# Row sums and weight norms in PSUM, and an f32 low rank stage for two attentions

## The chip, the cores and the metric

One core of one Trainium2 chip. The metric is the device time of one execution in microseconds (us), the median of the runs. The core has TensorE (matmuls; PE in the rows, and PEld for its weight loads), VectorE (DVE), ScalarE (ACT), GpSimd (POOL) and SyncE (SP), whose queue issues the DMAs here. Each of them takes its instructions in order. [...]

## The reference

Three blocks in a row, in f32, on a batch of 4, 448 positions and 768 channels (12 heads of 64):

```python
x = attention(q, k, v)                        # causal softmax(q k^T / 8) v, 12 heads
xt = x.transpose(0, 2, 1)                     # "moe": low rank mixing of the positions, then an MLP
u = x + (xt @ U @ V).transpose(0, 2, 1)       # U (448, 32), V (32, 448)
x = u + np.maximum(u @ w_ch1, 0) @ w_ch2      # 768 -> 3072 -> 768
# "moe2": gate, top 2 of 4 experts; an expert is a causal attention of one head of 64, times wo
out = sum_e gate[e] * (softmax(q_e k_e^T / 8) v_e) @ wo[e]
```

## The kernel before

Positions are cut into NC = 4 chunks of C = 112, channels into KD = 6 blocks of 128, so that a block is a pair of heads. Accuracy comes from pairs of f16 numbers: an operand is cut into a high part and a rest, and a product is three f16 matmuls (`PASS`: high by high, high by rest, rest by high). The scores q k^T are f32 matmuls.

An attention (`attention(b)`, batch b) runs over its six pairs of heads, n = 6 b + p. For each: `softmax` forms the scores, takes row maxima under the mask on VectorE, exponentials with their row sums on ScalarE (`SUS`, 112 x 8: two heads by four chunks), cuts the result into high part (ScalarE) and rest (GpSimd), and transposes both by two DMA transposes. `weighted` calls `shares`, in which VectorE turns the eight sums per row into reciprocals, cuts these into two f16 parts and TensorE spreads them over the 64 rows of each head; then it multiplies the probabilities with v, and VectorE scales the product by the shares: y, 128 channels by 448 positions, in X3. ScalarE and GpSimd cut y into `XHL`, for the low rank stage.

`lowrank(n)`, issued a pair later: a DMA transpose turns XHL into XTR (positions in the partitions), twelve f16 matmuls of 128 columns multiply it by `U3` (U in high part and rest, three copies side by side, 96 columns), ScalarE scales the result out of the bank, VectorE subtracts on 32 of the 96 partitions, so that high part and rest stand above each other, and one f16 matmul by `VST` gives the addend, which VectorE adds to X3. For b = 0 the sum is cut into UH and UL at once.

Weights of the MLP arrive as f64; `weight_pair` decodes two tiles with integer operations on VectorE (three of 768 elements per tile), squares them on ScalarE, sums the squares with one f32 matmul into a bank (`norm`, 128 x 2), forms a power of two from it in four small VectorE operations and cuts the tiles, with two GpSimd subtractions of 384 columns each per tile. The MLP itself (`mlp(g, bs)`) runs in four groups of weights; the line `ORDER` says in which order attentions (a), MLP groups (m), joint groups (s) and experts (e) are written: a0 m00 a1 m01 m101 m20 m30 e0 a2 and so on.

All operations are first collected in `Program` and given a key; `plan` simulates the engines and issues the ready operation with the smallest key on each, after `SHIFTS` moved the keys of each part. Up to a fixed time, and at the end, it fills planned gaps of TensorE with dummy matmuls (`prog.idle`, L1346, 448 columns into bank 7) that keep its clock up; nothing uses their result.

`psum(kind)` hands out banks in turn: "b" (shares) and "l" (low rank) both take banks 3 and 4, "o" (weighted) bank 2, "r" (norm) bank 7, "s" (scores) 0 and 1. Every operation is recorded through one helper, so that nearly all instructions carry its line, L365; they are told apart by engine, operation and shape.

Of the kernel before, what the change touches and what calls it, by code (L numbers as in the profile page):

```python
# [20 lines left out]
NP = H // 2  # L21
# [347 lines left out]
def kernel(  # L369
# [96 lines left out]
    XHL = [view("xhl", i * 2048, 128, F16, 1024).rearrange("p (l s) -> p l s", l=2) for i in range(2)]  # L466
# [3 lines left out]
    U3 = view("u3", 0, 128, F16, 2 * NC * 3 * R).rearrange("p (l c r) -> p l c r", l=2, c=NC)  # L470
# [53 lines left out]
    def bits(a):  # L524
        return a.bitcast(I32)
# [127 lines left out]
    def shares(y, coef=None):  # L653

        i = heads[0] // 2 % 2
        su, rc = SUS[1 - i], RCH[1 - i]
        dve.tensor_scalar(su, su, EPS, 1.0 / RSC, op0=ALU.add, op1=ALU.mult)
# [7 lines left out]
        t = psum("b")  # L665
# [8 lines left out]
    def weighted(vs, pts, y, dst, coef=None, kind="o"):  # L674
# [13 lines left out]
        act.activation(dst[:, 0, 0:S], y, AF.Copy)  # L688
        pool.tensor_tensor(out=dst[:, 1, 0:S], in0=y, in1=dst[:, 0, 0:S], op=ALU.subtract)

    def lowrank(n):
        b, p = divmod(n, NP)
        iv = IV[:, b:b + 1]
        tst = TST
        sp.dma_start_transpose(out=XTR, in_=XHL[n % 2].rearrange("p l s -> p (l s)"))
        t = psum("l")
        with prog.group():
            for c in range(NC):
                for i, (lu_, lx) in enumerate(PASS):
                    mm(t[0:96, 0:128], U3[:, lu_, c], XTR[:, 4 * lx + c], c == 0 and i == 0, c == NC - 1 and i == 2)  # L700
# [74 lines left out]
    def attention(b):  # L775
        if b == B - 1:
            prog.key = HT * 30
            zero_pads(SLOTS[b][1][2:])
        if not b:
            prog.key = HT * 0.4  # L780
            v_scale(b)
            bound(CAP, SCAP, PV[:, 0:1])
# [486 lines left out]
    for a in XHL:  # L1269
        dve.memset(a[:, :, S:512], 0.0)  # L1270
# [122 lines left out]
```

## Time and profile before

| | |
|---|---|
| median of 3 runs | 1044.56 us (1044.13 to 1045.81) |
| profiled execution | 1046.19 us, of which the span of the trace is 1044.5 |
| granted clock of TensorE, mean | 0.994 |
| busy: TensorE, VectorE, ScalarE, GpSimd | 1024.4 (98%), 692.0 (66%), 613.6 (59%), 458.5 us (44%) |
| dummy matmuls among TensorE's | 383, 85.2 us |
| DMA | 192.53 MB, 88 DMA transposes |

The durations of the rows come from the one profiled execution, so they add up to its span and not to the median. A matmul's row shows its whole way through the array; how fast matmuls follow each other is read from the starts of neighbouring rows. In the rows "arena" is SBUF, "bank" PSUM, and out<-in (shape<-shape) are an instruction's operands; an f32 matmul has two records.

### The profile page before, as it was taken

The page shows a single profiled execution, that of the slowest core. Times are in us where ns is not written, and L with a number is a line of the kernel's source. Part 1 is how long each engine was busy: PE and PEld are TensorE (multiplying, and loading weights), DVE is VectorE, ACT ScalarE, POOL GpSimd, SP SyncE. Part 2 cuts the span into 40 slices and gives each one's busy share as a digit, 9 for nine tenths or more (in the row PEclk, how much of TensorE's full clock was granted, in tenths as well). Part 3 has the DMA queues.
Part 4 walks back from the last instruction along what each step waited for, and adds up shares of the span by engine and source line. Part 5 has one row for each costly group of instructions (what it writes and reads, how often), then busy time and mean ns, then how long its engine had stood idle before and what let it go on. Part 6 is the DMA issues. An engine that isn't in the chain of part 4 may idle for free.

```text
span 1044.5 us, 18607 instructions
## 1 busy us (share of the span) xinstructions
PE 1024.4 (98%) x6724; PEld 543.7 (52%) x6724; DVE 692.0 (66%) x1744; ACT 613.6 (59%) x1470; POOL 458.5 (44%) x500
## 2 busy tenths in 40 slices
PE   9999999999998999999999999999999999999998
PEld 4454555555544445644555644455555555655554
DVE  8888899876767677555647556488655677522363
ACT  6899886657744563668662569674552632722173
POOL 3777763343433331235540137567796891310011
PEclk9999999999998999999999999999999999999999
DMA  9999998566787887269994269893435445453024
GB/s 245 225 219 237 239 246 259 182 233 232 254 289 259 278 299 265 80 155 224 236 251 118 70 158 214 218 194 112 132 100 166 136 136 163 109 136 106 18 75 102
DMA packets 220139, 192.53 MB, mean 184 GB/s; under 512 B 176304, under 2 KB 179504, under 8 KB 220048
## 3 DMA queue, kind: packets, MB, share of 16 engines
q1 hardware_dynamic: 220048, 191.36, 68.1%
q8 instruction: 52, 0.85, 0.3%
q14 instruction: 39, 0.32, 0.1%
HBM read 112.16 MB, written 36.18 MB: 142 GB/s over the span
## 4 chain that ended last, share of the span: by engine, by line
PE 58%; DMA 4%; ACT 1%; POOL 1%; DVE 1%; issue 0%; SPq 0%; ACTq 0%; POOLq 0%
PE bank L365 58%; DMA arena<-arena 2%; ACT arena L365 1%; DMA out_dram<-arena 1%; DMA arena<-in_v_dram 1%; POOL arena L365 1%; DVE arena L365 1%; PE bank L1346 0%; ACT bank L365 0%; SPq L365 0%; ACTq L365 0%; POOLq L365 0%
## 5 line engine op out<-in xcount | busy, mean ns | idle before, releaser
L365 PE MATMUL bank<-arena 128*128 128x448 f16 (+12 forms) x6341 | 949.5, 326 | 14.6 <-ACT arena L365 7.8
L365 POOL TENSOR_TENSOR arena<-arena 128x384 f16<-128x384 f32 (+8 forms) x493 | 457.5, 949 | 575.0 <-ACT arena L365 506.6
L365 PEld LDWEIGHTS <-arena 128*128 128x128 f16 (+4 forms) x5853 | 473.5, 105 | 407.6 <-issue 62.6
L365 ACT ACTIVATE arena<-arena 128x448 f16<-128x448 f32 (+12 forms) x872 | 476.9, 585 | 214.7 <-DVE arena L365 122.1
L365 DVE SCALAR_TENSOR_TENSOR arena<-arena 128x768 int32<-128x768 int32 (+7 forms) x193 | 176.7, 930 | 6.3 <-ACT arena L365 5.0
L365 DVE TENSOR_TENSOR arena<-bank,arena 128x448 f16<-128x448 f32 (+2 forms) x160 | 95.5, 600 | 109.3 <-ACT arena L365 87.3
L365 DVE CUSTOM_DVE_ANT_0 arena<-bank,arena 112x112 f32<-112x112 f32 (+4 forms) x280 | 124.2, 477 | 62.5 <-PE bank L365 52.1
L365 DVE SCALAR_TENSOR_TENSOR arena<-bank,arena 128x448 f32<-128x448 f32 (+1 forms) x138 | 84.7, 621 | 66.1 <-PE bank L365 59.1
L365 DVE TENSOR_SCALAR arena<-arena 128x1 f32<-128x1 f32 (+11 forms) x305 | 81.7, 294 | 44.3 <-ACT arena L365 17.8
L365 ACT ACTIVATE bank<-bank,arena 128x448 f32<-128x448 f32 x72 | 43.1, 599 | 105.0 <-PE bank L365 105.0
L365 ACT ACTIVATE arena<-bank 128x448 f16<-128x448 f32 (+2 forms) x148 | 76.0, 518 | 48.3 <-PE bank L365 47.1
L365 DVE TENSOR_TENSOR arena<-arena 112x8 f16<-112x8 f32 (+10 forms) x136 | 86.2, 647 | 26.4 <-ACT arena L365 24.5
L1346 PE MATMUL bank<-arena 128*128 128x448 f16 x383 | 85.2, 360 | 1.8 <-DVE arena L1263 1.0
L365 ACT ACTIVATE arena<-bank,arena 128x448 f32<-128x448 f32 (+2 forms) x73 | 33.0, 458 | 57.9 <-PE bank L365 53.0
L365 PEld LDWEIGHTS bank<-arena 64*112 64x112 f32 (+4 forms) x488 | 39.6, 171 | 46.4 <-issue 16.7
L365 DVE TENSOR_REDUCE arena<-arena 128x1 f32<-128x448 f32 (+8 forms) x107 | 57.3, 545 | 5.7 <-DMA arena<-in_v_dram 2.3
L1346 PEld LDWEIGHTS <-arena 128*128 128x128 f16 x383 | 35.4, 101 | 42.7 <-issue 15.0
L365 ACT ACTIVATION_READ_ACCUMULATOR arena<-arena 112x1 f32 (+1 forms) x304 | 57.3, 188 | 0.0
L365 DVE DVE_READ_ACCUMULATOR2_ANT arena<- 112x1 f32 (+1 forms) x280 | 23.0, 82 | 0.0
L365 DVE CAST arena<-arena 112x8 f16<-112x8 f32 x32 | 9.0, 285 | 3.0 <-PE bank L365 2.7
L365 DVE TENSOR_SCALAR arena<-bank 128x2 f32<-128x2 f32 x24 | 3.7, 153 | 9.4 <-PE bank L365 9.3
L365 DVE RECIPROCAL arena<-arena 112x8 f32<-112x8 f32 (+1 forms) x36 | 7.0, 195 | 0.6
(11 smaller groups left out, 13.8 us busy)
## 6 DMA issues: line engine op xcount, KB each, us to landing
arena<-w SPq DMA_DIRECT2D x138, 384.0 KB, 3.4
arena<-in_w_dram SPq DMA_DIRECT2D x48, 768.0 KB, 5.5
w<-arena SPq DMA_DIRECT2D x78, 384.0 KB, 5.0
arena<-in_qk_dram SPq DMA_DIRECT2D x24, 448.0 KB, 4.8
arena<-in_v_dram SPq DMA_DIRECT2D x24, 224.0 KB, 4.6
out_dram<-arena SPq DMA_DIRECT2D x24, 224.0 KB, 2.1
arena<-in_we_dram SPq DMA_DIRECT2D x6, 384.0 KB, 6.4
arena<-arena SPq DMA_TRANSPOSE x88, 4.8
```

Source lines behind the costliest of these rows:

```text
L365: fn(*a, **k)
L1346: prog.idle = lambda late: nc.tensor.matmul(bank[:, 0 if late else 7, 64:512], ZERO.to_broadcast([128, 128]), ZERO.to_broadcast([128, S]), ...
```

## The change

- `norm`: the first and the third of the four small VectorE operations on the weight norm write the bank instead of SBUF, and the second and the fourth read it.
- `shares`: the bank for the spread shares is claimed first, and columns 448 to 455 of it hold the eight sums per row from the first VectorE operation on; the reciprocal, the product with the gates' weights, the cast and the subtraction read them there.
- For b < 2 (`lowrank32`): no cut of y into XHL, no DMA transpose, no U3. TensorE transposes y in four f32 matmuls against the identity, ScalarE copies the bank into `XNF` (112 x 512, f32); four f32 matmuls by U (`UF`, 32 columns) accumulate, ScalarE copies 32 x 128 to `TSF`, one f32 matmul by V (`LV`) gives the addend. The end of the stage (`finish`) is as before. For b >= 2 the stage stays f16, with 112 instead of 128 partitions.
- U is loaded in four blocks of 112 rows and not 128; the pads of XHL are zeroed ahead of attention 2 and not at the start; UF, LV and TSF lie where the expert weights `wv` come later, not in the ring of weight tiles.
- `SHIFTS` has new values, so the order of all engines' instructions is new.

```diff
@@ -49,31 +49,29 @@
 NT = 2 * NG * GF + NE
 MOVABLE = 270000.0
 SHIFTS = (
...
 )
 PASS = [(0, 0), (0, 1), (1, 0)]
 
@@ -463,11 +461,15 @@
         (P32[0:3], PHL[0:2], PT[0:3]),
         (P32[0:3], PHL[0:2] + [hslot("hid", 10752 + 5120 * i) for i in range(2)], PT[0:3]),
     ]
-    XHL = [view("xhl", i * 2048, 128, F16, 1024).rearrange("p (l s) -> p l s", l=2) for i in range(2)]
+    XHL = [view("xhl", i * 2048, 128, F16, 1024).rearrange("p (l c x) -> p l c x", l=2, c=NC) for i in range(2)]
+    XNF = [view("xhl", i * 2048, C, F32, 512) for i in range(2)]
+    LV = view("wv", 0, 96, F32, S)
+    UF = view("wv", 1792, C, F32, NC * R)
+    TSF = [view("wv", 2304 + 512 * i, R, F32, 128) for i in range(2)]
     XTR = view("xtr", 0, 128, F16, 1024).rearrange("p (k e) -> p k e", k=8)
     TST = view("tst", 0, 96, F16, 128)
     MASK = view("mask", 0, C, BF16, S)
-    U3 = view("u3", 0, 128, F16, 2 * NC * 3 * R).rearrange("p (l c r) -> p l c r", l=2, c=NC)
+    U3 = view("u3", 0, C, F16, 2 * NC * 3 * R).rearrange("p (l c r) -> p l c r", l=2, c=NC)
     ID = view("id", 0, 128, F16, 128)
     IDF = view("idf", 0, 128, F32, 128)
     ONE = view("one", 0, 128, F32, 128)
@@ -653,8 +655,10 @@
     def shares(y, coef=None):
 
         i = heads[0] // 2 % 2
-        su, rc = SUS[1 - i], RCH[1 - i]
-        dve.tensor_scalar(su, su, EPS, 1.0 / RSC, op0=ALU.add, op1=ALU.mult)
+        rc = RCH[1 - i]
+        t = psum("b")
+        su = t[0:C, S:S + 8]
+        dve.tensor_scalar(su, SUS[1 - i], EPS, 1.0 / RSC, op0=ALU.add, op1=ALU.mult)
         dve.reciprocal(su, su)
         if coef is not None:
             v = su.rearrange("p (h c) -> p c h", h=2)
@@ -662,7 +666,6 @@
         su = su.rearrange("p (h c) -> p h c", h=2)
         dve.tensor_copy(rc[:, 0], su)
         dve.tensor_tensor(out=rc[:, 1], in0=su, in1=rc[:, 0], op=ALU.subtract)
-        t = psum("b")
         with prog.group():
             for c in range(NC):
                 for l in range(2):
@@ -685,24 +688,54 @@
                            pt[0:C, k:k + kc * (NC - 1 - j) + 1:kc],
                            i == 0 and j == 0, i == 2 and j == NC - 1)
         dve.tensor_tensor(out=y, in0=t[:, 0:S], in1=y, op=ALU.mult)
-        act.activation(dst[:, 0, 0:S], y, AF.Copy)
-        pool.tensor_tensor(out=dst[:, 1, 0:S], in0=y, in1=dst[:, 0, 0:S], op=ALU.subtract)
+        if len(dst.shape) == 2:
+            t = psum("l")
+            with prog.group():
+                for c in range(NC):
+                    mm(t[0:C, 128 * c:128 * c + 128], y[:, C * c:C * c + C], IDF, True, True)
+            act.activation(dst, t[0:C], AF.Copy)
+            return
+        if len(dst.shape) == 4:
+            hi, lo = [dst[:, l, :, 0:C] for l in range(2)]
+            y = y.rearrange("p (c x) -> p c x", c=NC)
+        else:
+            hi, lo = dst[:, 0, 0:S], dst[:, 1, 0:S]
+        act.activation(hi, y, AF.Copy)
+        pool.tensor_tensor(out=lo, in0=y, in1=hi, op=ALU.subtract)
+
+    def lowrank32(n):
+        b, p = divmod(n, NP)
+        t = psum("l")
+        with prog.group():
+            for c in range(NC):
+                mm(t[0:R, 0:128], UF[:, R * c:R * c + R], XNF[n % 2][:, 128 * c:128 * c + 128], c == 0, c == NC - 1)
+        act.activation(TSF[n % 2], t[0:R, 0:128], AF.Copy)
+        u = psum("l")
+        mm(u[:, 0:S], TSF[n % 2], LV[0:R], True, True)
+        finish(n, u)
 
     def lowrank(n):
         b, p = divmod(n, NP)
-        iv = IV[:, b:b + 1]
+        if b < 2:
+            lowrank32(n)
+            return
         tst = TST
-        sp.dma_start_transpose(out=XTR, in_=XHL[n % 2].rearrange("p l s -> p (l s)"))
+        sp.dma_start_transpose(out=XTR, in_=XHL[n % 2].rearrange("p l c x -> p (l c x)"))
         t = psum("l")
         with prog.group():
             for c in range(NC):
                 for i, (lu_, lx) in enumerate(PASS):
-                    mm(t[0:96, 0:128], U3[:, lu_, c], XTR[:, 4 * lx + c], c == 0 and i == 0, c == NC - 1 and i == 2)
+                    mm(t[0:96, 0:128], U3[:, lu_, c], XTR[0:C, 4 * lx + c], c == 0 and i == 0, c == NC - 1 and i == 2)
         act.activation(tst, t[0:96, 0:128], AF.Copy, scale=CT[0:96])
         dve.scalar_tensor_tensor(out=tst[32:64], in0=t[32:64, 0:128], scalar=CT[32:64], in1=tst[32:64],
                                  op0=ALU.mult, op1=ALU.subtract)
         u = psum("l")
         mm(u[:, 0:S], tst, VST, True, True)
+        finish(n, u)
+
+    def finish(n, u):
+        b, p = divmod(n, NP)
+        iv = IV[:, b:b + 1]
         dve.tensor_tensor_reduce(out=X3[b][:, p], in0=u[:, 0:S], in1=X3[b][:, p], scale=iv, scalar=BIG,
                                  op0=ALU.add, op1=ALU.max, accum_out=TOP)
         k = b * KD + p
@@ -776,6 +809,10 @@
         if b == B - 1:
             prog.key = HT * 30
             zero_pads(SLOTS[b][1][2:])
+        if b == 2:
+            prog.key = HT * 30
+            for a in XHL:
+                dve.memset(a[:, :, :, C:128], 0.0)
         if not b:
             prog.key = HT * 0.4
             v_scale(b)
@@ -795,7 +832,7 @@
             softmax([[(QK[i][64 * j:64 * j + 64, 1], QK[i][64 * j:64 * j + 64, 0])] for j in range(2)], -0.125,
                     pts, slots=SLOTS[b][0:2])
             prog.key = HT * (2 * n + 1)
-            weighted([VH[:, 2 * i + j] for j in range(2)], pts, X3[b][:, p], XHL[i])
+            weighted([VH[:, 2 * i + j] for j in range(2)], pts, X3[b][:, p], XNF[i] if b < 2 else XHL[i])
             if p:
                 prog.key = HT * (2 * n - 1)
                 lowrank(n - 1)
@@ -843,10 +880,10 @@
             act.activation(hi, t, AF.Square, scale=2.0 ** -20, accum_out=am[:, j:j + 1])
         norm = psum("r")[:, 0:2]
         mm(norm, ONE, am, True, True)
-        dve.tensor_scalar(s, norm, FLOOR2, None, op0=ALU.max)
-        dve.tensor_scalar(bits(p), bits(s), 1, HALFM, op0=ALU.logical_shift_right, op1=ALU.bitwise_and)
-        dve.tensor_scalar(bits(s), bits(p), HALFM, None, op0=ALU.bitwise_xor)
-        dve.tensor_scalar(s, s, 2.0 ** 57, None, op0=ALU.mult)
+        dve.tensor_scalar(norm, norm, FLOOR2, None, op0=ALU.max)
+        dve.tensor_scalar(bits(p), bits(norm), 1, HALFM, op0=ALU.logical_shift_right, op1=ALU.bitwise_and)
+        dve.tensor_scalar(bits(norm), bits(p), HALFM, None, op0=ALU.bitwise_xor)
+        dve.tensor_scalar(s, norm, 2.0 ** 57, None, op0=ALU.mult)
         for j, k in enumerate(ks):
             hi, lo = tiles[i + j]
             t = DEC[(i + j) % 4]
@@ -1239,10 +1276,9 @@
 
     HT = 4500.0
     dve.memset(view("sm", 0, 128, F32, SM), 0.0)
-    UR = view("ring", 0, 128, I32, 2 * NC * R)
-    US = view("ring", 2048, 128, F32, NC * R)
+    UR = view("ring", 0, C, I32, 2 * NC * R)
+    US = UF
     VR = view("ring", 4096, 96, I32, 2 * S)
-    LV = view("ring", 8192, 96, F32, S)
     load_pair(0)
     prog.key = HT * 0.2
     load_v(0)
@@ -1266,13 +1302,11 @@
         prog.key = HT * 0.2
         load_v(n)
     prog.key = HT * 0.3
-    for a in XHL:
-        dve.memset(a[:, :, S:512], 0.0)
     zero_pads(PHL[0:2] + SPARE)
     prog.key = HT * 0.3
     decode(US, UR)
     decode(LV, VR)
-    absmax(TMP[:, 5:6], US)
+    absmax(TMP[0:C, 5:6], US)
     absmax(TMP[0:96, 6:7], LV)
     PUV, SUV = DC[:, 0:2], DC[:, 2:4]
     reduce_all(TMP[:, 5:7], PUV, SUV)
@@ -1290,7 +1324,7 @@
     U3V = U3.rearrange("p l c (i r) -> p l c i r", i=3)
     USV = US.rearrange("p (c r) -> p c r", c=NC)
     for r in range(3):
-        split(U3V[:, 0, :, r], U3V[:, 1, :, r], USV, SUV[:, 0:1])
+        split(U3V[:, 0, :, r], U3V[:, 1, :, r], USV, SUV[0:C, 0:1])
     act.activation(VST, LV, AF.Copy, scale=SUV[0:96, 1:2])
     dve.scalar_tensor_tensor(out=VST[64:96], in0=LV[64:96], scalar=SUV[64:96, 1:2], in1=VST[64:96],
                              op0=ALU.mult, op1=ALU.subtract)
@@ -1362,7 +1396,7 @@
     hosts = {
         "qk": qk.transpose(1, 2, 3, 5, 0, 4).reshape(B, NP, 128, 2, S),
         "v": x["v"].reshape(B, NP, 2, NC, C, HD).transpose(0, 1, 4, 2, 3, 5).reshape(B, NP, C, 512),
-        "lu": _np.pad(x["moe_U"], ((0, 64), (0, 0))).reshape(NC, 128, R).transpose(1, 0, 2).reshape(128, NC * R),
+        "lu": x["moe_U"].reshape(NC, C, R).transpose(1, 0, 2).reshape(C, NC * R),
         "lv": x["moe_V"],
         "w1": x["moe_w_ch1"].reshape(KD, 128, NG, GF, 128).transpose(2, 3, 1, 0, 4).reshape(NG, GF, 128, 768),
         "w2": x["moe_w_ch2"].reshape(NG, GF, 128, KD, 128).transpose(0, 3, 2, 1, 4).reshape(NG, KD, 128, 768),
```

## Rows read from the trace of the kernel before

**Rows 1.** Busy time by stretch: us, PE, PEld, DVE, ACT, POOL; clock, DMA share, GB/s.

```profile
0.00:20.00 20.00, 19.00 (x106) 8.73 (x106) 15.86 (x80) 11.09 (x34) 7.79 (x16) 1.00 0.96 273
20.00:140.00 120.00, 117.83 (x977) 60.92 (x974) 106.53 (x343) 108.87 (x323) 82.24 (x99) 1.00 1.06 227
140.00:180.00 40.00, 38.35 (x285) 21.12 (x284) 36.97 (x73) 28.05 (x51) 18.95 (x20) 1.00 1.00 269
300.00:390.00 90.00, 81.87 (x412) 41.44 (x411) 61.73 (x108) 48.25 (x79) 29.54 (x29) 0.94 0.82 276
```

**Rows 2.** The same of the dummy matmuls alone: us, PE, PEld, clock, DMA share, GB/s.

```profile
0.00:20.00 20.00, 13.81 (x58) 5.61 (x58) 1.00 0.96 273
20.00:140.00 120.00, 56.02 (x255) 23.22 (x256) 1.00 1.06 227
140.00:180.00 40.00, 7.27 (x34) 3.00 (x32) 1.00 1.00 269
...
1000.00:1045.00 45.00, 8.12 (x38) 3.60 (x38) 0.98 0.38 88
sum 1045.00, PE 85.22 PEld 35.43; mean PE 12.17 PEld 5.06
```

**Rows 3.** Timeline of weight loads: start us, us, engine, line, operation, shape, count.

```profile
126.89 0.47 PEld L365 LDWEIGHTS bank<-arena 64*112 64x112 f32 x8
127.84 0.72 PEld L365 LDWEIGHTS <-arena 128*96 128x96 f16 x12 [0.48 <-issue]
128.49 0.30 PEld L365 LDWEIGHTS bank<-arena 128*128 128x128 f32 x2
```

**Rows 4.** Timeline of matmuls: an f32 group of 448 columns and what follows.

```profile
123.91 1.01 PE L365 MATMUL bank<-arena 64*112 64x448 f32 x4
124.85 0.56 PE L1346 MATMUL bank<-arena 128*128 128x448 f16 x2
```

**Rows 5.** Timeline of matmuls: the last product of the low rank stage and what follows.

```profile
130.47 0.35 PE L365 MATMUL bank<-arena 96*128 96x448 f16 x1
130.67 0.55 PE L1346 MATMUL bank<-arena 128*128 128x448 f16 x2
```

**Rows 6.** Groups by shape, 0 to 180 us: busy us, mean ns | idle before, releaser.

```profile
L365 POOL TENSOR_TENSOR arena<-arena 128x448 f16<-128x448 f32 x12 | 12.5, 1041 | 2.4 <-ACT arena L365 2.2
...
L365 ACT ACTIVATE arena<-arena 128x448 f16<-128x448 f32 x18 | 10.7, 597 | 0.8 <-DVE arena L365 0.8
...
L365 DVE TENSOR_TENSOR arena<-arena 112x8 f16<-112x8 f32 x12 | 7.5, 625 | 0.0
...
L365 DVE TENSOR_SCALAR arena<-arena 112x8 f32<-112x8 f32 x12 | 5.2, 437 | 1.4 <-ACT arena L365 1.3
...
L365 DVE SCALAR_TENSOR_TENSOR arena<-bank,arena 32x128 f16<-32x128 f32 x12 | 4.1, 344 | 2.9 <-ACT arena L365 2.6
...
L365 DVE CAST arena<-arena 112x8 f16<-112x8 f32 x12 | 3.5, 296 | 0.0
...
L365 DVE TENSOR_SCALAR arena<-arena 128x2 int32<-128x2 int32 x13 | 3.3, 254 | 0.0
...
L365 DVE TENSOR_SCALAR arena<-bank 128x2 f32<-128x2 f32 x6 | 0.9, 154 | 1.3 <-PE bank L365 1.1
```

**Rows 7.** Who waited for whom, 20 to 180 us: total us, times, longest.

```profile
ACT arena L365 <- DVE arena L365: 12.4, 15, 3.5
...
DVE arena L365 <- PE bank L365: 8.7, 19, 0.9
...
PE bank L1346 <- DVE arena L365: 0.8, 3, 0.3
```

**Rows 8.** Timeline of all engines, 111 to 120 us, two rows of it.

```profile
113.08 1.69 DVE L365 TENSOR_TENSOR arena<-arena 112x8 f16<-112x8 f32 x1
...
117.89 1.82 PE L365 MATMUL bank<-arena 128*96 128x128 f16 x20 [0.82 <-DMA arena<-arena]
```

**Rows 9.** DMA issues on the page: count, median us from issue to landing.

```profile
arena<-arena SPq DMA_TRANSPOSE x88, 4.8
```

48 rows, old and new, of the table SHIFTS are left out of this document.

## The prediction

> **What bounds the kernel now.** I read the busy time by stretch first, then the dummy matmuls alone, then the groups of the first 180 us, then who waits for whom there. By stretch, TensorE looks full everywhere [rows 1], but part of that is made: the line of the dummies holds 13.81 + 56.02 + 7.27 = 77.1 us of the first 180 us, none between 180 and 1000, and 8.1 us at the end [rows 2]. With the idle rest of the first three stretches (1.00 + 2.17 + 1.65 = 4.8 us) TensorE has 82 us to spare before 180 us and almost nothing behind (8.1 us idle between 300 and 390, the clock at 0.94 there). So the kernel is in two parts: up to 180 us, attentions 0 and 1 and the decoding of the first weights, paced by other engines; behind it a stream of matmuls that TensorE itself paces. The end moves by as much as the first part gets shorter, plus whatever real TensorE work no longer fits under the dummies.
>
> What paces the first part: between 20 and 140 us VectorE is busy for 106.5 of 120 us (89%) and ScalarE for 108.9 (91%); between 140 and 180 VectorE 37.0 of 40 (92%), ScalarE only 28.1, and TensorE has just 7.27 + 1.65 = 8.9 us of dummies and idle time [rows 1, 2]. Two engines near their limit, and one that is near it at the end.
>
> **TensorE: what is added.** Per head pair of attentions 0 and 1, the old low rank stage is twelve f16 matmuls of 128 columns, 127.84 to 128.49 = 0.65 us [rows 3], and one of 448 columns, 130.47 to 130.67 = 0.20 us [rows 5]: 0.85 us. New: four f32 transposes of 128 columns, four f32 matmuls of 128 columns and one f32 matmul of 448. An f32 group of 448 columns takes 123.91 to 124.85 = 0.94 us [rows 4] (two heads beside each other in the rows of the array); split over two stationary operands of 112 and 336 columns it takes 126.89 to 127.84 = 0.95 us [rows 3], so a second stationary operand costs next to nothing. That is 2.1 ns per column, 0.27 us for 128. Sum: 4 x 0.27 + 4 x 0.27 + 0.94 = 3.1 us, 2.2 us more per pair, 27 us for twelve. [...] I take 27, since the group with two operands is the nearest row. Its cover is the 82 us; where that is gone each pair costs its 2.2 us in full. One pair passes in about 160 / 12 = 13.3 us, so three to four fall into 140 to 180: 6.6 to 8.8 us against 8.9 us to spare. It just fits, with nothing left for waits in TensorE's order; I charge 1 us there.
>
> **VectorE: what goes.** The subtraction on 32 partitions goes from twelve pairs: 12 x 0.344 = 4.1 us [rows 6]. The small operands move to PSUM. An operation on eight elements that reads and writes SBUF averages 625 ns (subtract), 437 (scale) and 296 (cast), and one of two integers 254, while the one of two elements that reads a bank takes 154 [rows 6]. One of these eight-element subtractions stood 1.69 us while GpSimd ran [rows 8]; operations with a bank among their operands show no such excess. At 154 each the twelve pairs give back 12 x (471 + 283 + 142) ns = 10.8 us, and the twelve integer steps of the first six weight pairs 1.2 us. With the 4.1 that is 16 us at most. At least it is 4.1: the stall may simply pass to the next operation that needs the port, a decode of 768 integers. I take 12, nearer to the upper end, because GpSimd loses 12 x 1.041 = 12.5 us of subtractions too [rows 6], so there are fewer stalls to pass on. The same savings behind 180 us are worth nothing: TensorE paces that part.
>
> [...] Here the row with the bank operand is the shortest of the small ones, so by the trace nothing is added.
>
> **GpSimd, ScalarE, DMA.** ScalarE's copy of 448 columns from SBUF, 597 ns [rows 6], becomes one of 512 from a bank: 682 if it goes by columns, 1.0 us over twelve pairs, and nothing or a little less than now if a bank is quicker to read. Its copy of the 96 rows gets smaller. I take nothing, so ScalarE keeps its 108.9 us. Twelve DMA transposes go, each 4.8 us from issue to landing [rows 9], and with them the waits in which a matmul at TensorE's head stands for one: 0.82 us at 117.89, with ScalarE and VectorE queued behind [rows 8]. SP, which waits for GpSimd's subtraction before it can issue such a transpose, no longer holds back the loads behind it.
>
> **What the new waits do.** Dummies write bank 7, and three of them waited for VectorE's read of the weight norm there, 0.8 us together [rows 7]. Now VectorE keeps that bank over four operations with others between them; at, say, 2 us for each of six pairs the dummies stand 12 us, which costs nothing while only dummies are queued, and is bounded by 12 us if matmuls are. I take 0. The row sums claim bank 3 or 4 before TensorE is ready to write it; that is a rival, below. The later place of the zeroing of pads and the smaller load of U: under 0.5 us, hidden.
>
> **The sum.** If ScalarE goes from 91% to 97% in the 120 us stretch, it shrinks to 108.9 / 0.97 = 112.3: 7.7 us. VectorE, with about 8 of its 12 us saved there, then stands at 98.5 of 112, and follows. 140 to 180 gives nothing, and I charge 1 us. Net 6.7 us. The profiled execution took 1046.2 us (1044.5 of span and 1.7 around it), the median of the three runs is 1.6 lower: 1046.2 - 6.7 - 1.6 = 1038. The new order may also move the holes between 300 and 390 us (8.1 us idle [rows 1]) and the last stretch either way; I take 0, and about 4 us either way for the range: 1032 to 1042 for this case.
>
> **Rivals.** *VectorE alone is the bound.* All 16 us go, at 91%: 17.6 us, and TensorE still has 82 - 27 - 18 = 37 us of dummies: 1046.2 - 17.6 - 1.6 = 1027. For it: 92% at the end of the first part, and a ScalarE that spent 12.4 us waiting for VectorE [rows 7]. Against it: ScalarE's 91%.
>
> *It does not do what it says.* The stalls pass to the decodes, only 4.1 us go, and TensorE's full last stretch (1 us charged, up to 2.2 us per pair if a dummy is not where the f32 work falls) eats them: 1044, within 0.2% of before, which is about what a measurement of this kernel can tell from no change.
>
> *Slower: two banks with too many tenants.* Row sums, the old product and its result share banks 3 and 4, in turn. Now the transposes come as a fourth tenant, and the row sums hold their bank from VectorE's first small operation on. A claim that finds its bank taken stands at VectorE's head for up to a tenancy, 1.07 us of f32 matmuls and 0.53 of ScalarE's copy, 1.6 us; behind it stand the maxima of the next scores and the decodes, and ScalarE waits for those. VectorE's waits for a bank are now 8.7 us in 19 [rows 7], 0.46 each. At 1.6 us for each of twelve pairs it idles 19 us for the 12 saved: 7 us longer, 1046.2 + 7 - 1.6 = 1052. It decides from 1.0 us per pair on. Against it: an order can set other work ahead of the claim.
>
> **How the numbers follow.** Forecast 0.45 (1038), VectorE alone 0.13 (1027), no effect 0.14 (1044), banks 0.28 (1052). Faster is the first two, 0.58; same 0.14; slower 0.28. The range runs from 1027 to 1052: it takes in the centres of all cases, and leaves out their outer halves, under 2 in 10.
>
> **What would show it.** Right: dummies before 180 us near 82 - 27 - 7 = 48 us; the 32-partition subtraction 12 times, not 24; small operations on PSUM near 0.15 us without outliers; 76 DMA transposes; the last low rank product of attention 1 some 7 us earlier, and as much at the end; ScalarE at 95% or more between 20 and 135 us. Wrong: f32 groups of over 1.2 us for four; VectorE's waits for banks above 20 us in the first part; dummies that fall by 27 us and a first part as long as now.

## The result, and the profile after

The changed kernel takes 1031.9 us (median of four runs, 1029.5 to 1032.3) where the kernel before takes 1044.4 (four runs, 1042.4 to 1045.8): 0.9877 of it, interval 0.9854 to 0.9900, some 12.5 us less. The forecast was 6.4 us less. The profiled execution took 1031.5 us, 1029.8 of it span, against a span of 1044.5 before.

Busy time by stretch of the kernel after (us, PE, PEld, DVE, ACT, POOL; clock, DMA share, GB/s), and under it the same of the dummies alone (PE, PEld; clock, DMA share, GB/s). They answer to [rows 1, 2]:

```profile
20.00:140.00 120.00, 118.25 (x949) 64.56 (x949) 101.94 (x335) 110.42 (x323) 76.52 (x91) 1.00 0.98 227
140.00:180.00 40.00, 39.87 (x283) 22.05 (x280) 32.56 (x85) 27.51 (x57) 19.46 (x21) 1.00 0.87 238
300.00:390.00 90.00, 82.62 (x429) 41.98 (x428) 56.08 (x110) 49.74 (x82) 30.23 (x32) 0.98 0.77 272
...
0.00:20.00 20.00, 13.98 (x58) 5.58 (x59) 1.00 0.83 260
20.00:140.00 120.00, 30.72 (x139) 12.01 (x137) 1.00 0.98 227
140.00:180.00 40.00, 0.00 (x0) 0.00 (x0) 1.00 0.87 238
```

The dummies of the first 180 us fell from 77.1 to 44.7 us. TensorE's groups by shape over these 180 us tell what stands there now. From the kernel before, the old low rank stage and the real f16 matmuls of 448 columns (the MLP's; the dummies have a line of their own):

```profile
L365 PE MATMUL bank<-arena 128*96 128x128 f16 x144 | 10.2, 220 | 1.1 <-DMA arena<-arena 1.1
L365 PE MATMUL bank<-arena 96*128 96x448 f16 x12 | 4.3, 358 | 0.6 <-DVE arena L365 0.6
L365 PE MATMUL bank<-arena 128*128 128x448 f16 x157 | 33.0, 353 | 0.7 <-DVE arena L365 0.7
```

From the kernel after, the three f32 groups (U products, transposes, V products) and the MLP:

```profile
L363 PE MATMUL bank<-arena 112*32 112x128 f32 x96 | 12.7, 276 | 0.0
L363 PE MATMUL bank<-arena 128*112 128x128 f32 x96 | 12.7, 275 | 0.0
L363 PE MATMUL bank<-arena 32*128 32x448 f32 x24 | 12.2, 586 | 0.0
L363 PE MATMUL bank<-arena 128*128 128x448 f16 x197 | 42.2, 354 | 0.0
```

The account closes, for this one profiled execution. TensorE lost 32.4 us of dummies and 1.8 of idle time. In their place stand 37.6 - 14.5 = 23.1 us of f32 work, 42.2 - 33.0 = 9.2 us of MLP, and 1.9 of other work. So the MLP is 40 matmuls further at 180 us, and behind that point TensorE paces the kernel, so those 9.2 us come off the end. All of that lead is made before 140 us, where the dummies went from 69.8 to 44.7 us. Between 140 and 180 us the MLP loses 14 matmuls, since the f32 groups (4.2, 4.1 and 3.3 us there) now stand where the last dummies were; the MLP's group from 140 to 180 us, before and after:

```profile
L365 PE MATMUL bank<-arena 128*128 128x448 f16 x121 | 24.7, 352 | 0.7 <-DVE arena L365 0.7
L363 PE MATMUL bank<-arena 128*128 128x448 f16 x107 | 22.3, 353 | 0.0
```

Another 4.4 come between 300 and 390 us, where the clock is 0.98 for 0.94 (0.04 x 90 = 3.6) and TensorE idles 7.4 for 8.1. The rest of the 14.7 us between the two spans is 1.1.

The prediction named one more sign: the last low rank product of attention 1 should come some 7 us earlier. Its matmul ends at 178.9 us before and at 173.1 after, 5.8 us earlier.

The rows that the prediction looked at on VectorE, 0 to 180 us (busy us, mean ns), answer to [rows 6]:

```profile
L363 DVE TENSOR_TENSOR arena<-bank,arena 112x8 f16<-112x8 f32 x12 | 1.9, 160 | 0.1
L363 DVE TENSOR_SCALAR bank<-arena 112x8 f32<-112x8 f32 x12 | 1.9, 158 | 1.3 <-ACT arena L363 1.3
L363 DVE CAST arena<-bank 112x8 f16<-112x8 f32 x12 | 1.9, 158 | 0.0
...
L363 DVE RECIPROCAL bank<-bank 112x8 f32<-112x8 f32 x12 | 2.5, 205 | 0.0
```

625, 437 and 296 ns became 160, 158 and 158. Who waited for whom, 20 to 180 us (us, times, longest), answers to [rows 7]; ScalarE waits for VectorE as long as before:

```profile
DVE arena L363 <- PE bank L363: 15.9, 22, 3.0
ACT arena L363 <- DVE arena L363: 12.4, 7, 5.5
```

SP is the engine that the prediction did not open. Its transposes from 28 to 175 us (count: shortest/median/longest ns), before with two kinds of loads, then after:

```profile
L365 SPq DMA_TRANSPOSE arena<-arena x34: 1231/2654/6901, 29.6 to 168.1; - x34
L365 SPq DMA_DIRECT2D arena<-in_w_dram x12: 328/358/552, 27.9 to 172.9; - x12
L365 SPq DMA_DIRECT2D arena<-in_v_dram x12: 332/528/1720, 34.7 to 164.9; - x12
```

```profile
L363 SPq DMA_TRANSPOSE arena<-arena x22: 2309/3559/7271, 29.6 to 155.2; - x22
```

Rows of its timeline before (start, us) show what that is at its worst; loads of queries, values and weights are queued behind:

```profile
118.55 8.20 SPq L365 DMA_TRANSPOSE arena<-arena  x3
126.84 0.53 SPq L365 DMA_DIRECT2D arena<-in_qk_dram  x1
127.47 0.39 SPq L365 DMA_DIRECT2D arena<-in_w_dram  x1
127.95 9.13 SPq L365 DMA_TRANSPOSE arena<-arena  x3
137.14 1.05 SPq L365 DMA_DIRECT2D arena<-in_v_dram  x2
```

### The profile page after: what moved, and what is told of

Read it like the earlier page. It is cut to its first block, busy times and chain, and to the rows that moved or that the text cites. A ratio compares the mean times of both kernels' runs of the same rounds, so it can differ in the third digit from the quotient of the medians.

```text
span 1029.8 us, 18366 instructions
## 1 busy us (share of the span) xinstructions
PE 1013.3 (98%) x6635; PEld 542.7 (53%) x6635; DVE 662.2 (64%) x1732; ACT 612.9 (60%) x1470; POOL 444.6 (43%) x488
## 4 chain that ended last, share of the span: by engine, by line
PE 59%; DMA 2%; ACT 2%; DVE 1%; issue 1%; POOL 0%; DVEq 0%; ACTq 0%; POOLq 0%
PE bank L363 59%; DMA arena<-arena 2%; ACT arena L363 1%; DVE arena L363 1%; POOL arena L363 0%; PE bank L1380 0%; ACT bank L363 0%; DVE bank L363 0%; DVEq L363 0%; ACTq L363 0%; POOLq L363 0%
## 5 line engine op out<-in xcount | busy, mean ns | idle before, releaser
L363 PE MATMUL bank<-arena 128*128 128x448 f16 (+13 forms) x6401 | 966.5, 327 | 11.9 <-DVE arena L363 5.5
L363 POOL TENSOR_TENSOR arena<-arena 112x448 f16<-112x448 f32 (+8 forms) x481 | 443.5, 944 | 574.9 <-ACT arena L363 489.1
L363 PEld LDWEIGHTS <-arena 128*128 128x128 f16 (+3 forms) x5697 | 462.2, 104 | 405.8 <-issue 62.6
L363 ACT ACTIVATE arena<-arena 112x112 f16<-112x112 f32 (+12 forms) x860 | 472.3, 586 | 211.4 <-DVE arena L363 117.4
L363 DVE TENSOR_TENSOR arena<-bank,arena 128x448 f16<-128x448 f32 (+3 forms) x192 | 100.3, 527 | 114.7 <-ACT arena L363 91.7
L363 ACT ACTIVATE arena<-bank 128x448 f16<-128x448 f32 (+4 forms) x172 | 86.1, 505 | 55.9 <-PE bank L363 54.3
L363 PEld LDWEIGHTS bank<-arena 64*112 64x112 f32 (+8 forms) x704 | 63.1, 163 | 49.8 <-issue 21.7
L363 DVE TENSOR_TENSOR arena<-arena 128x448 f16<-128x448 f32 (+7 forms) x96 | 70.9, 754 | 24.4 <-ACT arena L363 23.2
L363 DVE TENSOR_SCALAR arena<-arena 128x1 f32<-128x1 f32 (+10 forms) x201 | 56.3, 310 | 34.1 <-DMA w<-arena 19.2
L363 DVE TENSOR_REDUCE arena<-arena 128x1 f32<-128x448 f32 (+7 forms) x107 | 57.6, 545 | 7.5 <-DMA arena<-in_v_dram 4.7
```

The costliest lines, as they stand in the source:

```text
L363: fn(*a, **k)
```

## The experiments

All ratios are to the kernel before on the same chip; "us" is the distance of the ratio from 1, times 1045. The order of the instructions is part of the code here, so there are two kinds of test: with an order held, and with one searched for the edited operations, by random changes of SHIFTS.

### Parts of the change undone, its order held

`same_order` and `same_order_2` are the changed kernel with its order written out, as the mark to compare with.

> The changed kernel itself, its order written out, as the base beside the three others on the same chip: every theory expects 0.988 of the kernel before.

> The changed kernel once more, as the base beside these two: 0.988 to 0.989 of the kernel before.

0.9893 (0.9841 to 0.9945) and 0.9877 (0.9839 to 0.9915): 11.2 and 12.9 us. Their profiled executions have 186 and 183 MLP matmuls by 180 us, where the one above has 197: one execution is good to some 14 matmuls, 3 us. In them the last low rank product of attention 1 ends at 175.1 and 175.9 us.

**Small operands back in SBUF** (`sums_sbuf`), row sums and weight norms:

```diff
-        su = t[0:C, S:S + 8]
+        su = SUB[1 - i]
...
-        dve.tensor_scalar(norm, norm, FLOOR2, None, op0=ALU.max)
+        dve.tensor_scalar(s, norm, FLOOR2, None, op0=ALU.max)
```

> The changed kernel (1031.9 us) with every engine's order held as it is, but the row sums and the weight norm worked on in SBUF again, as before. If VectorE's small operations pace the first part, about 12 us of stalls come back there (12 x 0.9 us of the row sums, 1.2 us of the norms): 1040 to 1044 us. If the gain is the order's, or the f32 stage's alone, it stays under 1034 us.

0.9897 (0.9865 to 0.9928), 10.8 us; `pool_back`, below, has 13.0 in the same comparison. The stalls are back in VectorE's groups:

```profile
L494 DVE TENSOR_TENSOR arena<-arena 112x8 f16<-112x8 f32 x12 | 6.1, 511 | 0.1
L494 DVE TENSOR_SCALAR arena<-arena 112x8 f32<-112x8 f32 x12 | 5.1, 429 | 0.7 <-ACT arena L494 0.7
L494 DVE CAST arena<-arena 112x8 f16<-112x8 f32 x12 | 3.7, 312 | 0.0
L494 DVE RECIPROCAL arena<-arena 112x8 f32<-112x8 f32 x12 | 2.3, 189 | 0.0
```

The first three alone are 14.9 us for 5.7. The kernel is 2 us behind `pool_back` by the ratios and 1 us by the medians (1036.9 and 1035.9), which is not clear of noise; a loss of the whole 12 us would lie outside the interval. The prediction's main term is real as busy time and small as time.

**GpSimd's subtraction back** (`pool_back`), as dead work beside ScalarE's new copy:

```diff
-            act.activation(dst, t[0:C], AF.Copy)
+            with prog.group():
+                act.activation(dst, t[0:C], AF.Copy)
+                pool.tensor_tensor(out=XTR.rearrange("p k e -> p (k e)")[:, 0:S], in0=y, in1=y, op=ALU.subtract)
```

> The changed kernel, order held, with twelve GpSimd subtractions of 128 x 448 put back, whose result nobody reads: 12.5 us of GpSimd, which hold the port that it shares with VectorE. If GpSimd's relief was worth something by itself, 1036 us or more; if the small operations no longer care for the port, the decodes alone stall a little and it is 1032 to 1035 us.

0.9876 (0.9833 to 0.9919): no cost shows; the interval would hide some 4 us.

**The DMA transposes back** (`dma_back`), dead too, of 896 columns where the old ones had 1024:

```diff
-            act.activation(dst, t[0:C], AF.Copy)
+            with prog.group():
+                act.activation(dst, t[0:C], AF.Copy)
+                sp.dma_start_transpose(out=XTR[:, 0:7], in_=WIDE)
```

> The changed kernel, order held, with twelve DMA transposes put back, each issued where y is copied, of 128 x 896 f16 zeros that nobody waits for: SP and the DMA engines have again what the old stage gave them, TensorE does not wait for it. If the transposes' place on SP and in the DMA engines was worth something, 1036 us or more; if only the engines' work counts, 1032 to 1034 us.

0.9991 (0.9966 to 1.0017): the whole gain is gone, 12 us for twelve transposes that nobody reads. Its waits from 20 to 180 us show by which way:

```profile
DVE arena L494 <- DMA arena<-in_v_dram: 9.5, 8, 2.0
PE bank L494 <- DMA arena<-arena: 9.4, 7, 2.1
```

In the kernel after the same two waits are 1.3 and 1.8 us. Loads of the values and the transposes that the kernel still needs come late; both go by SP's queue, in which the added ones stand. Rows of that queue in `dma_back` (start, us) leave hardly a gap:

```profile
141.49 7.32 SPq L494 DMA_TRANSPOSE arena<-arena  x2
148.92 0.65 SPq L494 DMA_DIRECT2D arena<-in_v_dram  x1
149.61 0.43 SPq L494 DMA_DIRECT2D arena<-in_w_dram  x1
150.14 5.61 SPq L494 DMA_TRANSPOSE arena<-arena  x1
155.85 0.52 SPq L494 DMA_DIRECT2D arena<-in_w_dram  x1
156.42 0.42 SPq L494 DMA_DIRECT2D arena<-in_v_dram  x1
```

Once issued, the loads of the values are about as quick as in the kernel after (28 to 175 us, after and then `dma_back`), so they come late because they are issued late:

```profile
DMA to landing us min/median/max: 2.8/3.7/7.1
DMA to landing us min/median/max: 2.8/3.9/7.5
```

Whether a transpose holds the queue by itself, or because the DMA engines behind it are full, this run does not separate: the engines' share of the first 180 us rises too, from 0.94 to 1.02. And up to 3.6 of the 12 us are clock, 0.98 of these 180 us in place of 1.00 (after, then `dma_back`):

```profile
0.00:180.00 180.00, 176.96 (x1315) 94.90 (x1316) 150.01 (x494) 149.35 (x412) 102.44 (x127) 1.00 0.94 233
0.00:180.00 180.00, 166.87 (x1239) 90.12 (x1240) 136.47 (x471) 144.37 (x402) 96.15 (x123) 0.98 1.02 228
```

**The f32 U products twice** (`f32_twice`), 11.9 us of TensorE as reckoned; in the trace their group grows by 10.5, from 12.7 to 23.2:

```diff
-            for c in range(NC):
+            for _ in range(2):
+                for c in range(NC):
...
```

> The changed kernel, order held, with the four f32 matmuls by U done twice in each of the twelve pairs: 12 x 0.99 = 11.9 us more on TensorE. If f32 work hides under the dummies (44.7 us before 180 us) except where there are none (from 140 us on, four pairs), it costs 4 us: 1036 us. If TensorE is the bound everywhere, 1044 us; if all hides, 1032 us.

0.9949 (0.9924 to 0.9974), 7.5 us more than the change's 0.9877, so some 0.6 to 0.7 of what is added reaches the end. The f32 work is not hidden by the dummies left.

**More VectorE, more ScalarE** (`dve_more`: the product with the reciprocals three times, 14.9 us more; `act_more`: the copy out of the bank three times, 14 us more):

```diff
-        dve.tensor_tensor(out=y, in0=t[:, 0:S], in1=y, op=ALU.mult)
+        with prog.group():
+            dve.tensor_tensor(out=y, in0=t[:, 0:S], in1=y, op=ALU.mult)
+            for _ in range(2 if len(dst.shape) == 2 else 0):
+                dve.tensor_tensor(out=XTR.rearrange("p k e -> p (k e)").bitcast(F32)[:, 0:S], in0=t[:, 0:S],
+                                  in1=y, op=ALU.mult)
...
-            act.activation(dst, t[0:C], AF.Copy)
+            with prog.group():
+                act.activation(dst, t[0:C], AF.Copy)
+                for _ in range(2):
+                    act.activation(XTR.rearrange("p k e -> p (k e)").bitcast(F32)[0:C], t[0:C], AF.Copy)
```

> The changed kernel, order held, with two more VectorE multiplications of 128 x 448 out of the bank in each of the twelve pairs, whose result nobody reads: 12 x 2 x 0.62 = 14.9 us more on VectorE in the first part. If VectorE paces that part, 12 us or more above the base; if SP's queue of DMA transposes paces it, under 5 us.

> The changed kernel, order held, with ScalarE's copy of the transposed rows done three times in each of the twelve pairs: 12 x 2 x 0.6 = 14 us more on ScalarE, which stands at 92% between 20 and 140 us. If ScalarE paces the first part, 12 us or more above the base; if SP's queue of DMA transposes paces it, under 5 us.

0.9929 (0.9906 to 0.9952) and 0.9927 (0.9898 to 0.9957): each costs some 4 us by `same_order` on the same chip and 5 by the change's 0.9877. A quarter to a third of what is added to either engine reaches the end; neither alone paces the first part.

### Work taken out of the old order

`no_dma` does not issue eleven of the twelve transposes of the low rank stage; `dve_less` leaves out the cast and subtraction of most row sums and the subtraction on 32 partitions, 13 us of VectorE as reckoned (the first 180 us have 9.9 less); `both_less` does both. The edit of `no_dma`, where `left_out` holds operations that keep their place in the order and are not issued:

```diff
         sp.dma_start_transpose(out=XTR, in_=XHL[n % 2].rearrange("p l s -> p (l s)"))
+        if 0 < n < 2 * NP:
+            prog.left_out.add(len(prog.ops) - 1)
```

> The kernel before, its order and all its engines' work as they are, with eleven of the twelve DMA transposes of the low rank stage of attentions 0 and 1 left out (the matmuls behind them read what the first one left, so the low rank addend of those pairs is wrong). If these transposes hold the first part up, 0.985 to 0.992 of the kernel before, with no f32 matmul and no PSUM operand in it; if VectorE's stalls or the order gave the gain, 0.996 or more.

> The kernel before and its order, with 13 us of VectorE's work left out of attentions 0 and 1: the cast and the subtraction of the row sums in ten pairs (10 x 0.92 us) and the subtraction on 32 partitions in twelve (12 x 0.34 us); the shares and the addend of these pairs are wrong. If VectorE paces the first part in the old order, 0.990 or less; if SP or several engines together do, 0.995 or more.

> The kernel before and its order, with both left out, eleven DMA transposes and 13 us of VectorE's work. If it takes both together to get out of the old order what the change gets, 0.988; if the old order itself holds the first part up, 0.993 or more.

0.9984 (0.9959 to 1.0010), 0.9981 (0.9963 to 1.0000), 0.9983 (0.9958 to 1.0008): some 2 us each and no more together, with intervals that reach 1, so not clear of no gain, and some 4 us at most. So `dma_back` must not be read backwards. Twelve transposes that an order has no room for cost 12 us; eleven taken out of an order that has room for them give little or nothing.

**The new operations in the old order** (`old_order`): the changed kernel with the priorities of the kernel before.

> The changed kernel's operations with the shifts of the kernel before, each taken over by its engine and its place in the program. If the operations alone carry the gain, 0.99 or less; if it lies in the order found for them, it is no faster than before, 1.0 to 1.015.

1.0080 (1.0047 to 1.0114), 8 us slower than before. By 180 us it has 18 of the 24 records of the V products:

```profile
L364 PE MATMUL bank<-arena 32*128 32x448 f32 x18 | 9.1, 586 | 0.0
```

### Each half with an order searched for it

`f32_alone` is the f32 stage with the small operands left in SBUF; `sums_alone` is the small operands in PSUM with the f16 stage left as it was; `no_dma_new` is `no_dma` with an order of its own.

> The f32 stage for attentions 0 and 1 alone: row sums and weight norms stay in SBUF as before, and the order is found anew for these operations. If the twelve DMA transposes are what the change gives, it has nearly all of the gain: 0.987 to 0.992 of the kernel before. If VectorE's small operations give it, 0.996 or more.

> The kernel before with only the small operands of the row sums and the weight scales in PSUM, and an order searched for these operations; the low rank stage, its DMA transposes and its f16 halves stay. By the prediction's VectorE theory (some 11 us of VectorE time less) 6 us or so faster than before, 0.994. By the theory that the transposes on SP's queue and the long low rank stage set the pace, within 2 us of before, 0.998 to 1.002. A bank that is held longer by the row sums could cost time, up to 1.004.

> As the run with eleven DMA transposes left out (the low rank addend of those pairs is wrong, no f32 matmul, small operands in SBUF), but with an order found anew for these operations. If the room that the transposes leave on SP is worth something only to an order made for it, 0.990 to 0.995 of the kernel before; if the transposes don't matter, 0.998 or more again.

`f32_alone` 0.9909 (0.9881 to 0.9937), 9.5 us faster than before. `sums_alone` 1.0030 (1.0009 to 1.0051), 3 us slower. `no_dma_new` 0.9961 (0.9940 to 0.9982), 4 us faster. The first two are the verdict on the theory of the prediction. Busy time of the first 180 us in `sums_alone` (us, PE, PEld, DVE, ACT, POOL):

```profile
0.00:180.00 180.00, 175.26 (x1359) 90.86 (x1360) 146.18 (x488) 150.02 (x408) 113.04 (x136) 1.00 0.97 236
```

VectorE has 159.4 - 146.2 = 13.2 us less to do there than before, what the prediction wanted, and the kernel is no faster. Nor is the first part shorter: the last low rank product of attention 1 ends at 178.6 us, against 178.9 before, and at 171.8 in `f32_alone`. MLP matmuls by 180 us, `sums_alone` and then `f32_alone`:

```profile
L367 PE MATMUL bank<-arena 128*128 128x448 f16 x168 | 36.4, 353 | 0.0
```

```profile
L366 PE MATMUL bank<-arena 128*128 128x448 f16 x192 | 41.6, 354 | 0.0
```

`sums_alone` gives its 11 more matmuls back behind 180 us, where it has 5.28 us of dummies and the kernel before has none.

### Is it one lucky order?

Two more orders for exactly the operations of the change: `order_2` searched on from the order of the change, `order_3` from that of the kernel before, from which `sums_alone` and `f32_alone` were searched too.

> The instructions of the changed kernel, in another order that was searched for them, starting from the order of the changed kernel. If the gain of 12 us hangs on one lucky order, this one loses several us of it; if it belongs to the operations and any order fitted to them has it, it lands within about 3 us of the changed kernel, at a ratio to before of 0.986 to 0.991.

> The instructions of the changed kernel, in an order that was searched for them starting from the order of the kernel before, without any use of the order that came with the change. If the gain belongs to the operations with any order fitted to them, 0.985 to 0.992 of before, against 1.008 for the old order unsearched. If it is the particular order of the change that brings it, 0.995 or more.

0.9820 (0.9793 to 0.9848) and 0.9836 (0.9809 to 0.9862). All three orders fitted to the new operations have the gain, so it belongs to the operations, and an order is needed to collect it. The same kind of search from the same start gave 1.0030 for the small operands alone, so a search does not bring the gain by itself; no run has a new order for the operations of the kernel before. `order_2`, 1026.3 us median, is faster than both kernels, 19 us below before. Most of what it adds lies between 300 and 390 us:

```profile
300.00:390.00 90.00, 86.65 (x462) 44.76 (x461) 60.56 (x113) 51.55 (x82) 25.85 (x28) 1.00 0.76 273
```

86.65 us busy at clock 1.00 where the change has 82.62 at 0.98: 4.0 and 1.8 us.

### The transposes in TensorE's transposing form

`pe_transpose` is the change with its order held and the f32 transposes as such, not as products with an identity:

```diff
-                    mm(t[0:C, 128 * c:128 * c + 128], y[:, C * c:C * c + C], IDF, True, True)
+                    mm(t[0:C, 128 * c:128 * c + 128], y[:, C * c:C * c + C], IDF, True, True, is_transpose=True)
```

> The changed kernel, order held, with the four f32 transposes of each pair issued in TensorE's transposing form instead of as f32 matmuls against the identity. [...] If TensorE's f32 work is hidden, no difference.

0.9847 (0.9811 to 0.9882), against 0.9877 for `same_order_2` beside it: some 3 us, with intervals that overlap. The group of transposes from 0 to 180 us:

```profile
L494 PE MATMUL bank<-arena 128*112 128x128 f32 x48 | 7.3, 275 | 0.0
```

12.7 us became 7.3, with one record for each where the product leaves two. At the 0.6 of `f32_twice` the 5.4 us would be worth 3 at the end, which fits, though this run alone is not clear of noise.

## Why the prediction was right in sign and wrong in size

**TensorE's account: right.** Dummies before 180 us were to fall to 48 and fell to 44.7. The f32 work was put at 27 us more and is 23.1, with the old stage counted by the same rows. The estimate of 3.1 us per pair holds: 37.6 / 12 = 3.1. What was too low is the old stage, 0.85 us by the starts of its weight loads, 14.5 / 12 = 1.2 by its groups.

**"VectorE: what goes", and "The sum": the steps that failed.** That the stalls vanish was right: the three operations went from 16.2 us to 5.7, 10.5 of the 10.8 reckoned, and the 4.1 on 32 partitions went too. That these us pace the first part was wrong. `sums_alone` is rid of the stalls and is 3 us slower, `sums_sbuf` has them again and loses at most a few us, `dve_more` adds 15 and loses 4 to 5. A share of 89% was read as a limit, but an engine at 89% that is waited for 12.4 us in 160 before and after [rows 7] is late now and then, not full. By the same step ScalarE was to go from 91% to 95% or more: it is at 110.42 of 120, 92%. The first part got shorter with its engines hardly denser than before. What it gained is near the 6.7 us of the sum all the same: 9.2 us of MLP work in the change, 7.1 and 6.4 in `same_order` and `same_order_2`, and a low rank stage that ends 5.8, 3.8 and 3.0 us earlier. That is luck, since the VectorE time that the sum was made of brings next to nothing by itself; it is the f32 stage that brings it, by `f32_alone`.

**"GpSimd, ScalarE, DMA": the term that was missing.** The twelve transposes entered with a wait of 0.82 us, and SP with a clause and no price. SP was never read as an engine: its queue carries every load and every transpose in turn, and 34 transposes hold it for a median of 2.65 us each. With an order of their own, leaving them out gives 4 us; in the new order, putting them back takes 12. The time from issue to landing does not show this: in the first 180 us before, its medians are 5.2 us for the transposes and 4.6 to 5.8 for the loads. The queue's rows do: there a plain load holds it for a median of 0.36 to 0.53 us.

**"140 to 180 gives nothing, and I charge 1 us": near.** All 7.27 us of dummies went there, f32 work took their place, and the MLP lost 24.7 - 22.3 = 2.4 us. With the old order the f32 work ran past this stretch, and the kernel was 8 us slower.

**300 to 390 us: a term put at 0 that is 4.4 in the profiled executions** (some 3.3 in the two copies), about the 4 us either way that the range gave it. With the first part near the forecast, this is the largest part of what the sum left out. It is a stall and what follows it. Before, in steps of 4 us (us, PE busy; clock, DMA share, GB/s):

```profile
320.00:324.00 4.00, 1.10 (x6) 0.84 0.91 209
324.00:328.00 4.00, 4.00 (x12) 0.50 1.01 412
328.00:332.00 4.00, 4.00 (x18) 0.80 0.74 246
```

TensorE stands 2.9 of 4 us, and then runs at a granted clock of 0.50, with 12 matmuls in 4 us where the full steps at 1.00 between 300 and 388 us have 22 to 24. Before has two such dips there, the change one, `order_2` none. The first 180 us, with the dummies, stand at 1.00; no run leaves the dummies out, so what they do for the clock is not shown apart.

**The rivals.** *VectorE alone is the bound* is refuted with the main theory. *No effect* and *banks* did not come: VectorE's waits for a bank did rise, from 8.7 us in 19 to 15.9 in 22 (the mark in the prediction was 20), without deciding. For a bank as an operand the prediction added nothing, by its row of 154 ns. The traces have 205 ns for the reciprocal in a bank and 189 in SBUF (`sums_sbuf`), where it meets no stalls: 16 ns more, and 0.2 us over twelve.

**What stays open.** The f32 stage with its order gives 9.5 us, and of that its transposes on SP give 4 by `no_dma_new`, if the two runs, each with an order of its own, may be subtracted. The other 5.5 are with the 4.1 us subtraction on 32 partitions, the shorter chain from the scaled rows to the V product, or an order that happened to be better; these were not taken apart. Whether the small operands add anything to the f32 stage is within the scatter: 0.9909 (0.9881 to 0.9937) without them, 0.9877 (0.9854 to 0.9900) with them.

## What to carry to other kernels

Ask of a busy engine what its freed time would start, and test it by adding dead work: here 15 us more on either "full" engine cost 4 to 5, while twelve dead transposes on the DMA queue cost 12. Read the issuing queue as an engine, with durations, as soon as loads share it with transposes. Where the order is part of the code, an edit is only measured with an order of its own: the f32 stage gave 9.5 us with one, while the new code in the old order was 8 us slower than before, and transposes left out gave 4 us with one and at most some 4, perhaps nothing, without.

## What the runs showed of the hardware

- The subtraction, scaling and cast of 8 elements in each of 112 partitions take VectorE 158 to 160 ns with a bank among their operands, and 296 to 625 ns on average in SBUF, beside a busy GpSimd. In the first 180 us before, ten of these 36 operations take 456 to 3567 ns, and each of the ten ends 23 to 32 ns after an instruction of GpSimd (the longest runs from 149.13 to 152.70 us, GpSimd's instructions beside it to 152.66); the thirteen with no GpSimd instruction beside them take at most 173 ns. In the kernel after, 25 of the 36 have GpSimd beside them and none takes over 170. The 24 longer decoding operations on 768 integers before take 901 to 1866 ns, those without GpSimd beside them at most 960. What the prediction calls the port shows in the rows as this wait. The reciprocal shows no such stalls: 205 and 189 ns.
- An f32 transpose of 128 columns as a product with an identity stands in the trace as two matmul records, in the transposing form as one: twelve groups of four take 12.7 and 7.3 us.
- A DMA transpose between places in SBUF holds SP's queue for 1.2 to 7.3 us, a plain load from in_w or in_v for 0.33 to 1.72.
